# A two-layer Mish MLP on one core: x tiles 0 and 1 as two loads, w1's first eight f tiles as four loads by k, and k 0 by single x tiles

## The chip, the cores and the metric

The kernel runs on one core of a Trainium2 chip. Its engines are TensorE (PE, with PEld for its weight loads), VectorE (DVE), ScalarE (ACT), GpSimd (POOL) and SyncE (SP). SP and ACT each issue DMAs on a ring of their own; the transfers of both run on the same 16 DMA engines. The metric is the time of one execution in device microseconds (us), lower is better.

## The reference

All inputs are bf16: x is [1, 2048, 512], w1 [512, 1792], b1 [1792], w2 [1792, 512].

```
h   = einsum("bsd,df->bsf", x, w1) + b1
sp  = log1p(exp(-abs(h))) + where(h > 0, h, 0)
act = h * tanh(sp)                       # Mish
out = einsum("bsf,fd->bsd", act, w2)
```

## The kernel before

The 512 of the first contraction are four **k tiles** of 128, the 1792 hidden columns fourteen **f tiles** of 128, and the 2048 rows of x sixteen **x tiles** of 128, taken in four blocks of four. For every block the kernel computes h transposed (f on the partitions), `mm1_step` multiplying w1's tile (k, f) with the transposed x; ScalarE applies Mish with the bias and writes `a_sb`; `mm2` multiplies `a_sb` with w2 over the fourteen f tiles, VectorE copies the result to `o_sb` and SP stores it. The last tile's 512 output columns are cut into 416 and 96, the 96 copied and stored by ScalarE.

x has to be transposed. For x tiles 2 to 15 transposing loads do that (`load_xT`). Tiles 0 and 1 come as they are into `x_nat`, and TensorE transposes them against an identity, eight pieces of 128 x 128 into PSUM, from where VectorE copies them to `xT` (`transpose_x`). One load brings both tiles, with two neighbouring rows of x on each partition, so 2 KB in one piece; the output rows of tiles 0 and 1 are taken in that interleaving (`x01`, `out01`).

The order on every engine is the order in which the program is written; `Stream.wait` puts a semaphore wait in front of the next instruction of an engine, and `Stream.mark` makes an instruction count up. SP issues the load of x, then w1's f tiles 0 to 3 and 4 to 7 (`GROUPS`), each as a load of k 0 and 1 and one of k 2 and 3, in pieces of 1 KB; the very first of those goes on ScalarE's ring instead, behind a wait for VectorE's memset of `b1_pad`. ScalarE then issues the load of b1. On SP follow xT for x tiles 2 and 3, w1's f tiles 8 to 13, w2, and xT of the other blocks. No load waits for anything.

TensorE begins with dummy matmuls on constants (`WARM`: five of 512 columns, five of 128) into PSUM bank 7. Then come the transposes (k 0, k 1, k 2 and 3, for both x tiles at once), then f tiles 0 to 3 and after them 4 to 7, k outermost in either group, each step with the 256 columns of x tiles 0 and 1; each f tile has a PSUM bank of its own number. Then the same eight f tiles with x tiles 2 and 3, f outermost, with Mish behind each; then f tiles 8 to 13 with 512 columns, `mm2` of block 0, and the other blocks.

Of the kernel before, what the change touches and what calls it, by code (L numbers as in the profile page):

```python
# [4 lines left out]

P = 128
WARM = (512,) * 5 + (128,) * 5
GROUPS = ((0, 4), (4, 8), (8, 14))
BLOCKS = (512, 512, 512, 512)
LAST = 96  # L10

# [22 lines left out]
def bass_standalone__dense_activation_mish__prompt_kernel(  # L34
# [10 lines left out]
    BF, F32 = dt.bfloat16, dt.float32  # L45
# [3 lines left out]
    KT, FT = D // P, F // P  # L49
    assert (S, D, F) == (2048, 512, 1792) and sum(BLOCKS) == S  # L50
    x2, out2 = x[0], out[0]
# [3 lines left out]
    F0 = 8  # L55

    with ExitStack() as es:
        def sb(name, shape, t):
            return es.enter_context(nc.sbuf_tensor(name, shape, t))

        x_nat = sb("x_nat", [P, 2, D], BF)
        xT = sb("xT", [P, KT, S], BF)
# [7 lines left out]
        ident = sb("ident", [P, P], BF)  # L70
        a_sb = sb("a_sb", [P, FT, S], BF)
        o_sb = sb("o_sb", [P, S // P, D], BF)
        ps = es.enter_context(nc.psum_tensor("ps", [P, 8, 512], F32))

        def sem(name):
            return es.enter_context(nc.semaphore(name))

        sp = Stream(nc.sync, None)
        pe = Stream(nc.tensor, sem("c_pe"))
        dve = Stream(nc.vector, sem("c_dve"))  # L80
        act = Stream(nc.scalar, sem("c_act"))
        pool = Stream(nc.gpsimd, sem("c_pool"))

        def load(q, dst, src, name, transpose=False):
            s = sem(name)
            (q.eng.dma_start_transpose if transpose else q.eng.dma_start)(dst, src).then_inc(s, 16)
            return (s, 16)

        t_w1, t_w2, t_xT = {}, {}, {}

        def load_w1(q, ks, a, b):
            t = load(q, w1_sb[:, ks, a * P:b * P], w1v[:, ks, a * P:b * P], "s_w1_%d_%d" % (ks.start, a))
            for f in range(a, b):
                for k in range(ks.start, ks.stop):
                    t_w1[k, f] = t

        def load_w2(a, b):
            t = load(sp, w2_sb[:, a:b, :], w2v[:, a:b, :], "s_w2_%d" % a)
            for f in range(a, b):
                t_w2[f] = t  # L100

        def load_xT(lo, hi):
            t = load(sp, xT[:, :, lo:hi], x2[lo:hi, :], "s_xT%d" % lo, True)
            for j in range(lo // P, hi // P):
                t_xT[j] = t

        t_bz = dve.mark(nc.vector.memset(b1_pad[:, :], 0.0))  # L107
        act.wait(t_bz)

        x01 = x2[0:2 * P, :].rearrange("(p j) d -> p j d", j=2)  # L110
        out01 = out2[0:2 * P, :].rearrange("(p j) d -> p j d", j=2)
        t_xn = load(sp, x_nat[:, :, :], x01, "s_xn")
        for a, b in GROUPS:
            if a == F0:
                load_xT(2 * P, 4 * P)
            for ks in (slice(0, 2), slice(2, KT)):
                load_w1(act if (a, ks.start) == (0, 0) else sp, ks, a, b)
        t_b1 = load(act, b1_nat[:, :], b1.rearrange("(j p) -> j p", p=P), "s_b1")
        load_w2(0, 5)
        load_w2(5, FT)  # L120
        for s in range(1, len(BLOCKS)):
# [4 lines left out]
        t_id = pool.mark(pool.eng.affine_select(ident[:, :], ones[:, :], pattern=[[1, P]], compare_op=ALU.is_equal,  # L126
                                                fill=0.0, base=0, channel_multiplier=-1))
# [5 lines left out]
        def dummy(n):  # L133
            nc.tensor.matmul(ps[:, 7, 0:n], c_w, c_m[:, 0:n], start=True, stop=True)  # L134

        free = [[] for _ in range(8)]
        t_cp = {}
        t_mish = {}


        def transpose_x(bank, ks):
            pe.wait(t_xn, t_id, *free[bank])
            psb = ps[:, bank, :].bitcast(BF)
            for i, k in enumerate(ks):
                for j in range(2):
                    mm = nc.tensor.transpose(psb[:, (2 * i + j) * P:(2 * i + j + 1) * P],  # L146
                                             x_nat[:, j, k * P:(k + 1) * P], ident[:, :])
            n = len(ks)
            dve.wait(pe.mark(mm))
            t = dve.mark(nc.vector.tensor_copy(xT[:, ks[0]:ks[0] + n, 0:2 * P],  # L150
                                               psb[:, 0:2 * n * P].rearrange("p (k t) -> p k t", k=n)))
            for k in ks:
                t_cp[k] = t
            free[bank] = [t]

        def mm1_step(s, f, k, bank, j0=0, j1=None):
            j1 = BLOCKS[s] // P if j1 is None else j1
            lo, hi = j0 * P, j1 * P
            first = k == 0 and j0 == 0
            if first:  # L160
                pe.wait(*free[bank])
            pe.wait(t_w1[k, f])
            for j in range(starts[s] // P + j0, starts[s] // P + j1):
                pe.wait(t_cp[k] if j < 2 else t_xT[j])
            return nc.tensor.matmul(ps[:, bank, lo:hi], w1_sb[:, k, f * P:(f + 1) * P],  # L165
                                    xT[:, k, starts[s] + lo:starts[s] + hi], start=first,
                                    stop=(k == KT - 1 and hi == BLOCKS[s]))
# [8 lines left out]
        s_out = sem("s_out")  # L176
        n_out = 0

        def put(i, lo, hi, bank, t_mm, q):
            nonlocal n_out  # L180
            if q is act:
                act.wait(t_mm)
                t = act.mark(act.eng.activation(o_sb[:, i, lo:hi], ps[:, bank, 0:hi - lo], ACT.Copy))  # L183
            else:
                dve.wait(t_mm)
                t = dve.mark(nc.vector.tensor_copy(o_sb[:, i, lo:hi], ps[:, bank, 0:hi - lo]))  # L186
            free[bank] = [t]
            q.wait(t)
            dst = out01[:, i, lo:hi] if i < 2 else out2[i * P:(i + 1) * P, lo:hi]
            q.eng.dma_start(dst, o_sb[:, i, lo:hi]).then_inc(s_out, 16)  # L190
            n_out += 1

        def mm2(i, lo, hi, bank, q=sp):
            s = max(b for b in range(len(BLOCKS)) if starts[b] <= i * P)
            pe.wait(*free[bank])
            for f in range(FT):
                pe.wait(t_w2[f], t_mish[s, f])
                mm = nc.tensor.matmul(ps[:, bank, 0:hi - lo], a_sb[:, f, i * P:(i + 1) * P], w2_sb[:, f, lo:hi],  # L198
                                      start=(f == 0), stop=(f == FT - 1))
            put(i, lo, hi, bank, pe.mark(mm), q)  # L200


        for n in WARM:
            dummy(n)
        transpose_x(6, (0,))
        transpose_x(5, (1,))
        transpose_x(4, (2, 3))
        dve.wait(t_b1, t_bz)
        t_b1p = dve.mark(nc.vector.tensor_copy(b1_pad[0:FT, :], b1_nat[:, :]))  # L209
        dve.wait(t_b1p)  # L210
# [1 line left out]
            t_b1t = dve.mark(nc.vector.transpose(b1_t[c * 32:(c + 1) * 32, :], b1_pad[:, c * 32:(c + 1) * 32]))  # L212
        dve.wait(t_b1t)
        t_b1c = dve.mark(nc.vector.tensor_copy(b1_sb[:, :], b1_t[:, 0:FT]))  # L214
        for a, b in GROUPS[:2]:
            for k in range(KT):
                for f in range(a, b):
                    mm1_step(0, f, k, f, 0, 2)
        for f in range(F0):
            for k in range(KT):  # L220
                mm = mm1_step(0, f, k, f, 2, 4)
            mish(0, f, f, pe.mark(mm))

        for s in range(len(BLOCKS)):
            for f in range(F0 if s == 0 else 0, FT):
                bank = f % 8 if s == 0 else 4 + f % 4
                for k in range(KT):
                    mm = mm1_step(s, f, k, bank)
                mish(s, f, bank, pe.mark(mm))
            for i in range(starts[s] // P, starts[s + 1] // P):  # L230
                if i < S // P - 1:
                    mm2(i, 0, D, i % 4)
                else:
                    mm2(i, 0, D - LAST, i % 4)
                    mm2(i, D - LAST, D, (i + 1) % 4, act)
# [29 lines left out]
```

## Time and profile before

| what | value |
|---|---|
| median of 3 runs | 105.43 us (105.28 to 105.50) |
| the profiled execution, own time | 105.59 us |
| its span, first to last instruction | 104.3 us |
| TensorE busy | 101.6 us, 97% of the span, 512 matmuls |
| ScalarE busy | 38.9 us (37%) |
| VectorE busy | 13.2 us (13%) |
| DMA | 7.94 MB in all |

The profiled execution's own time is 1.3 us longer than its span: that lies around the first and the last instruction. Busy times of TensorE include the time in which a matmul drains while the next one already runs, so a duration is more than the distance from one matmul to the next; the distance is read from counts in a stretch, or from how the duration grows with the columns. All times in rows are microseconds from the start of the span unless they are marked ns.

### The profile page before, as it was taken

The page shows a single profiled execution, that of the slowest core. Times are in us where ns is not written, and L with a number is a line of the kernel's source. Part 1 is how long each engine was busy: PE and PEld are TensorE (multiplying, and loading weights), DVE is VectorE, ACT ScalarE, POOL GpSimd, SP SyncE. Part 2 cuts the span into 40 slices and gives each one's busy share as a digit, 9 for nine tenths or more (in the row PEclk, how much of TensorE's full clock was granted, in tenths as well). Part 3 has the DMA queues.
Part 4 walks back from the last instruction along what each step waited for, and adds up shares of the span by engine and source line. Part 5 has one row for each costly group of instructions (what it writes and reads, how often), then busy time and mean ns, then how long its engine had stood idle before and what let it go on. Part 6 is the DMA issues. An engine that isn't in the chain of part 4 may idle for free.

```text
span 104.3 us, 1168 instructions
## 1 busy us (share of the span) xinstructions
PE 101.6 (97%) x512; PEld 50.0 (48%) x512; DVE 13.2 (13%) x26; ACT 38.9 (37%) x58; POOL 0.7 (1%) x6
## 2 busy tenths in 40 slices
PE   6999999999999999999999999999999999999992
PEld 2689744444444444444444444444444444444452
DVE  0340000022220000022220000022112000021222
ACT  1303998000027777200007777500005777700000
POOL 2000000000000000000000000000000000000000
PEclk9999999999999999999999999999999999999999
DMA  2999999981101000010111000001111000001111
GB/s 48 360 296 356 351 257 142 258 202 50 37 14 50 0 0 6 0 49 1 50 50 50 0 0 0 9 0 50 50 50 50 0 0 0 0 6 50 50 50 50
DMA packets 13377, 7.94 MB, mean 76 GB/s; under 512 B 7868, under 2 KB 13244, under 8 KB 13372
## 3 DMA queue, kind: packets, MB, share of 16 engines
q1 hardware_dynamic: 12928, 7.58, 27.6%
q10 hardware_dynamic: 444, 0.29, 0.9%
q8 instruction: 4, 0.07, 0.3%
q14 instruction: 1, 0.01, 0.0%
HBM read 3.94 MB, written 2.10 MB: 58 GB/s over the span
## 4 chain that ended last, share of the span: by engine, by line
PE 97%; ACT 0%; issue 0%
PE ps L165 47%; PE ps L198 46%; PE ps L134 3%; PE ps L146 1%; ACT o_sb L183 0%
## 5 line engine op out<-in xcount | busy, mean ns | idle before, releaser
L171 ACT ACTIVATE a_sb<-ps,b_sb 128x512 bf16<-128x512 f32 x56 | 37.4, 693 | 50.1 <-PE ps L165 50.1
L165 PE MATMUL ps<-xT,w_sb 128*128 128x512 bf16 (+1 forms) x256 | 50.0, 357 | 0.0
L198 PE MATMUL ps<-w_sb,a_sb 128*128 128x512 bf16 (+2 forms) x238 | 49.0, 366 | 0.0
L165 PEld LDWEIGHTS ps<-xT,w_sb 128*128 128x128 bf16 x256 | 25.4, 100 | 23.6
L198 PEld LDWEIGHTS ps<-w_sb,a_sb 128*128 128x128 bf16 x238 | 22.6, 98 | 26.1
L186 DVE CAST o_sb<-ps 128x512 bf16<-128x512 f32 (+1 forms) x16 | 11.0, 685 | 84.8 <-PE ps L198 84.8
L183 ACT ACTIVATE o_sb<-ps 128x96 bf16<-128x96 f32 x1 | 0.3, 251 | 11.4 <-PE ps L198 11.4
L134 PE MATMUL ps<-const-bfloat16-1.0 128*128 128x512 bf16 (+1 forms) x10 | 2.8, 469 | 0.8 <-PEq L250 0.8
L134 PEld LDWEIGHTS ps<-const-bfloat16-1.0 128*128 128x128 bf16 x10 | 1.2, 142 | 2.2 <-issue 2.2
L128 ACT ACT_TABLE_LOAD x1 | 1.3, 1283 | 2.2 <-issue 2.2
L150 DVE COPY xT<-ps 128x256 bf16<-128x256 bf16 (+1 forms) x3 | 0.9, 336 | 3.2 <-PE ps L146 3.1
L146 PE MATMUL ps<-ident,x_nat 128*128 128x128 bf16 x8 | 1.0, 311 | 0.0
L146 PEld LDWEIGHTS ps<-ident,x_nat 128*128 128x128 bf16 x8 | 0.8, 142 | 0.3 <-DMA x_nat<-in_x_dram 0.3
L212 DVE STREAM_TRANSPOSE b_t<-b_pad 32x32 bf16<-32x32 bf16 x4 | 0.8, 202 | 0.1
L126 POOL TENSOR_SCALAR_AFFINE_SELECT ident<-ones 128x128 bf16<-128x128 bf16 x1 | 0.3, 294 | 0.1
L107 DVE MEMSET b_pad<- 32x64 uint32 x1 | 0.1, 112 | 0.9 <-PEq L250 0.9
L124 POOL MEMSET ones<- 128x128 bf16 x1 | 0.2, 205 | 0.3 <-POOLq L250 0.3
L209 DVE COPY b_pad<-b_nat 14x128 bf16<-14x128 bf16 x1 | 0.2, 182 | 0.2 <-DMA b_nat<-in_b_dram 0.2
L214 DVE CAST b_sb<-b_t 128x14 f32<-128x14 bf16 x1 | 0.2, 175 | 0.0
L250 POOL MEMSET const-bfloat16-1.0<- 128x1 bf16 x1 | 0.1, 102 | 0.0
L250 POOL MEMSET const-uint8-127<- 128x1 uint8 x1 | 0.1, 102 | 0.0
L250 POOL MEMSET const-float32-0.0<- 128x1 f32 x1 | 0.1, 99 | 0.3 <-issue 0.3
(1 smaller groups left out, 0.1 us busy)
## 6 DMA issues: line engine op xcount, KB each, us to landing
out_dram<-o_sb SPq DMA_DIRECT2D x15, 128.0 KB, 1.7
w_sb<-in_w_dram SPq DMA_DIRECT2D x1, 1152.0 KB, 10.1
w_sb<-in_w_dram SPq DMA_DIRECT2D x3, 256.0 KB, 4.2
w_sb<-in_w_dram SPq DMA_DIRECT2D x2, 384.0 KB, 5.4
w_sb<-in_w_dram SPq DMA_DIRECT2D x1, 640.0 KB, 7.2
x_nat<-in_x_dram SPq DMA_DIRECT2D x1, 256.0 KB, 2.8
w_sb<-in_w_dram ACTq DMA_DIRECT2D x1, 256.0 KB, 3.4
out_dram<-o_sb SPq DMA_DIRECT2D x1, 104.0 KB, 1.7
```

The lines of the kernel that those rows point to most:

```text
L126: t_id = pool.mark(pool.eng.affine_select(ident[:, :], ones[:, :], pattern=[[1, P]], compare_op=ALU.is_equal, fill=0.0, base=0, channel_mu ...
L128: act.eng.preload_act_table(ACT.Mish)
L134: nc.tensor.matmul(ps[:, 7, 0:n], c_w, c_m[:, 0:n], start=True, stop=True)
L146: mm = nc.tensor.transpose(psb[:, (2 * i + j) * P:(2 * i + j + 1) * P], x_nat[:, j, k * P:(k + 1) * P], ident[:, :])
L150: t = dve.mark(nc.vector.tensor_copy(xT[:, ks[0]:ks[0] + n, 0:2 * P], psb[:, 0:2 * n * P].rearrange("p (k t) -> p k t", k=n)))
L165: return nc.tensor.matmul(ps[:, bank, lo:hi], w1_sb[:, k, f * P:(f + 1) * P], xT[:, k, starts[s] + lo:starts[s] + hi], start=first, stop=( ...
L171: t = act.mark(act.eng.activation(a_sb[:, f, starts[s]:starts[s + 1]], ps[:, bank, 0:BLOCKS[s]], ACT.Mish, bias=b1_sb[:, f:f + 1]))
L183: t = act.mark(act.eng.activation(o_sb[:, i, lo:hi], ps[:, bank, 0:hi - lo], ACT.Copy))
L186: t = dve.mark(nc.vector.tensor_copy(o_sb[:, i, lo:hi], ps[:, bank, 0:hi - lo]))
L198: mm = nc.tensor.matmul(ps[:, bank, 0:hi - lo], a_sb[:, f, i * P:(i + 1) * P], w2_sb[:, f, lo:hi], start=(f == 0), stop=(f == FT - 1))
L212: t_b1t = dve.mark(nc.vector.transpose(b1_t[c * 32:(c + 1) * 32, :], b1_pad[:, c * 32:(c + 1) * 32]))
L250: nc = _bacc.Bacc("TRN2", target_bir_lowering=False, num_devices=1)
```

## The change

x tiles 0 and 1 come as two loads on SP's ring, tile by tile, each with one row of x (1 KB) on a partition; the output rows of tiles 0 and 1 are then plain rows as those of the others. w1's f tiles 0 to 7 come as four loads, one for each k, in pieces of 2 KB: k 0 on ScalarE's ring, k 1 to 3 on SP's. `GROUPS` goes. `transpose_x` takes one x tile at a time and copies in four parts instead of three: x0's k 0, x0's k 1 to 3, x1's k 0, x1's k 1 to 3, in banks 4 to 7. Of the five dummies of 128 columns one is left (`GAP`), between the transposes of x0 and of x1. The steps on x tiles 0 and 1 run k outermost over all eight f tiles; k 0 runs over the eight f tiles with x0 alone (128 columns) and then with x1 alone, k 1 to 3 with both (256 columns).

```diff
-WARM = (512,) * 5 + (128,) * 5
-GROUPS = ((0, 4), (4, 8), (8, 14))
+WARM = (512,) * 5
+GAP = (128,)
...
-        x01 = x2[0:2 * P, :].rearrange("(p j) d -> p j d", j=2)
-        out01 = out2[0:2 * P, :].rearrange("(p j) d -> p j d", j=2)
-        t_xn = load(sp, x_nat[:, :, :], x01, "s_xn")
-        for a, b in GROUPS:
-            if a == F0:
-                load_xT(2 * P, 4 * P)
-            for ks in (slice(0, 2), slice(2, KT)):
-                load_w1(act if (a, ks.start) == (0, 0) else sp, ks, a, b)
+        def load_x(j):
+            t_xn[j] = load(sp, x_nat[:, j, :], x2[j * P:(j + 1) * P, :], "s_xn%d" % j)
+
+        load_x(0)
+        load_x(1)
+        for k in range(KT):
+            load_w1(sp if k else act, slice(k, k + 1), 0, F0)
         t_b1 = load(act, b1_nat[:, :], b1.rearrange("(j p) -> j p", p=P), "s_b1")
+        load_xT(2 * P, 4 * P)
+        for ks in (slice(0, 2), slice(2, KT)):
+            load_w1(sp, ks, F0, FT)
...
-        def transpose_x(bank, ks):
-            pe.wait(t_xn, t_id, *free[bank])
-            psb = ps[:, bank, :].bitcast(BF)
+        def transpose_x(j, bank, ks):
+            pe.wait(t_xn[j], t_id, *free[bank])
+            psb = ps[:, bank, 0:2 * P].bitcast(BF)
             for i, k in enumerate(ks):
-                for j in range(2):
-                    mm = nc.tensor.transpose(psb[:, (2 * i + j) * P:(2 * i + j + 1) * P],
-                                             x_nat[:, j, k * P:(k + 1) * P], ident[:, :])
+                mm = nc.tensor.transpose(psb[:, i * P:(i + 1) * P], x_nat[:, j, k * P:(k + 1) * P], ident[:, :])
...
-        transpose_x(6, (0,))
-        transpose_x(5, (1,))
-        transpose_x(4, (2, 3))
+        transpose_x(0, 4, (0,))
+        transpose_x(0, 5, (1, 2, 3))
+        for n in GAP:
+            dummy(n)
+        transpose_x(1, 6, (0,))
+        transpose_x(1, 7, (1, 2, 3))
...
-        for a, b in GROUPS[:2]:
-            for k in range(KT):
-                for f in range(a, b):
-                    mm1_step(0, f, k, f, 0, 2)
+        for j in range(2):
+            for f in range(F0):
+                mm1_step(0, f, 0, f, j, j + 1)
+        for k in range(1, KT):
+            for f in range(F0):
+                mm1_step(0, f, k, f, 0, 2)
```

TensorE's first rows, from the start of the program to the second block's first product; a minus is the kernel before, a plus the changed one (L134 and L135 are the dummies, L146 the transposes, L165 and L164 the steps on w1):

```order
-L134 MATMUL ps<-const-bfloat16-1.0 128x512 x5
-L134 MATMUL ps<-const-bfloat16-1.0 128x128 x5
-L146 MATMUL ps<-ident,x_nat 128x128 x8
-L165 MATMUL ps<-xT,w_sb 128x256 x64
...
+L135 MATMUL ps<-const-bfloat16-1.0 128x512 x5
+L146 MATMUL ps<-ident,x_nat 128x128 x4
+L135 MATMUL ps<-const-bfloat16-1.0 128x128
+L146 MATMUL ps<-ident,x_nat 128x128 x4
+L164 MATMUL ps<-xT,w_sb 128x128 x16
+L164 MATMUL ps<-xT,w_sb 128x256 x56
```

The transposes are in two parts with a dummy between them, and eight steps of 256 columns have become sixteen of 128.

What TensorE waits for there in the changed kernel (s_xn0 and s_xn1 are the loads of x0 and x1, s_w1_0_0 to s_w1_3_0 those of w1's k 0 to 3, c_dve the copies of VectorE):

```order
2 L146 MATMUL ps<-ident,x_nat 128x128 [waits c_pool,s_xn0]
3 L146 MATMUL ps<-ident,x_nat 128x128 x3
4 L135 MATMUL ps<-const-bfloat16-1.0 128x128
5 L146 MATMUL ps<-ident,x_nat 128x128 [waits s_xn1]
6 L146 MATMUL ps<-ident,x_nat 128x128 x3
7 L164 MATMUL ps<-xT,w_sb 128x128 [waits c_dve,s_w1_0_0]
8 L164 MATMUL ps<-xT,w_sb 128x128 x4
9 L164 MATMUL ps<-xT,w_sb 128x128 [waits c_dve] x3
10 L164 MATMUL ps<-xT,w_sb 128x128 x8
```

The wait for x1 stands ahead of every step on w1.

SP's first rows, the loads in the order of issue, before and after:

```order
-L86 DMA x_nat<-in_x_dram 128x1024
-L86 DMA w_sb<-in_w_dram 128x2x512 x3
+L86 DMA x_nat<-in_x_dram 128x512 x2
+L86 DMA w_sb<-in_w_dram 128x1024 x3
 L86 DMA_TRANSPOSE xT<-in_x_dram 128x4x256
 L86 DMA w_sb<-in_w_dram 128x2x768 x2
```

One load more stands ahead of xT's first, and the second place on the ring is x1's.

## Rows read from the trace of the kernel before

**Rows 1.** The page's busy times, us (share of the span) xinstructions.
```profile
PE 101.6 (97%) x512; PEld 50.0 (48%) x512; DVE 13.2 (13%) x26; ACT 38.9 (37%) x58; POOL 0.7 (1%) x6
```
**Rows 2.** The chain that ended last, pieces in order: start, length, what.
```profile
0.84 2.83 PE ps L134 x10
...
4.70 13.06 PE ps L165 x88
17.75 12.09 PE ps L198 x56
...
90.28 12.14 PE ps L198 x70
```
**Rows 3.** Who waited for whom: the one wait of TensorE for data.
```profile
PEld ps L146 <- DMA x_nat<-in_x_dram: 0.3, 1, 0.3
```
**Rows 4.** Timeline of the DMA issues on SP and ACT: start, length, line, operation.
```profile
0.81 0.39 SPq L86 DMA_DIRECT2D x_nat<-in_x_dram  x1
1.02 0.43 ACTq L86 DMA_DIRECT2D w_sb<-in_w_dram  x1
1.26 0.41 SPq L86 DMA_DIRECT2D w_sb<-in_w_dram  x1
1.72 0.46 SPq L86 DMA_DIRECT2D w_sb<-in_w_dram  x1
...
2.74 1.30 SPq L86 DMA_TRANSPOSE xT<-in_x_dram  x1
```
**Rows 5.** DMA issues, same order, and two stores: KB, us from issue to landing.
```profile
x_nat<-in_x_dram SPq DMA_DIRECT2D x1, 256.0 KB, 2.8
w_sb<-in_w_dram ACTq DMA_DIRECT2D x1, 256.0 KB, 3.4
w_sb<-in_w_dram SPq DMA_DIRECT2D x1, 256.0 KB, 3.9
w_sb<-in_w_dram SPq DMA_DIRECT2D x1, 256.0 KB, 4.2
...
xT<-in_x_dram SPq DMA_TRANSPOSE x1, 5.0
...
out_dram<-o_sb SPq DMA_DIRECT2D x15, 128.0 KB, 1.7
out_dram<-o_sb ACTq DMA_DIRECT2D x1, 24.0 KB, 1.6
```
**Rows 6.** TensorE's timeline around the transposes: the last dummy, transposes, first steps.
```profile
3.35 0.31 PE L134 MATMUL ps<-const-bfloat16-1.0 128*128 128x128 bf16 x1
3.66 1.03 PE L146 MATMUL ps<-ident,x_nat 128*128 128x128 bf16 x8
...
4.53 2.04 PE L165 MATMUL ps<-xT,w_sb 128*128 128x256 bf16 x9
```
**Rows 7.** By line and form, PE to 6.39, DVE to 7: busy us, mean ns.
```profile
L134 PE MATMUL ps<-const-bfloat16-1.0 128*128 128x512 bf16 x5 | 2.3, 624 | 0.8 <-PEq L250 0.8
L165 PE MATMUL ps<-xT,w_sb 128*128 128x256 bf16 x9 | 2.0, 411 | 0.0
...
L150 DVE COPY xT<-ps 128x256 bf16<-128x256 bf16 x2 | 0.5, 292 | 3.1 <-PE ps L146 3.1
L150 DVE COPY xT<-ps 128x512 bf16<-128x512 bf16 x1 | 0.4, 423 | 0.1
```
**Rows 8.** Stretches, L165 alone: length, PE busy (count), PEld, granted clock, DMA share, GB/s.
```profile
4.53:6.40 1.87, 1.87 (x9) 1.33 (x10) 1.00 1.15 337
6.40:8.02 1.62, 1.62 (x17) 1.46 (x15) 1.00 1.14 291
```
**Rows 9.** A stretch, PE: length, busy (count), granted clock, DMA share, GB/s.
```profile
1.75:2.50 0.75, 0.75 (x4) 1.00 0.90 134
```
**Rows 10.** Timeline: the last step on b1, and the first Mish.
```profile
6.48 0.17 DVE L214 CAST b_sb<-b_t 128x14 f32<-128x14 bf16 x1
...
9.62 0.69 ACT L171 ACTIVATE a_sb<-ps,b_sb 128x512 bf16<-128x512 f32 x1 [6.12 <-PE ps L165]
```

More of the change, by code (lines that the diff above doesn't have):

```diff
@@ L87, in load @@
             return (s, 16)
-        t_w1, t_w2, t_xT = {}, {}, {}
+        t_xn, t_w1, t_w2, t_xT = [None] * 2, {}, {}, {}
         def load_w1(q, ks, a, b):
@@ L138, in bass_standalone__dense_activation_mish__prompt_kernel @@
         t_mish = {}
-        def transpose_x(bank, ks):
-            pe.wait(t_xn, t_id, *free[bank])
-            psb = ps[:, bank, :].bitcast(BF)
+        def transpose_x(j, bank, ks):
+            pe.wait(t_xn[j], t_id, *free[bank])
+            psb = ps[:, bank, 0:2 * P].bitcast(BF)
             for i, k in enumerate(ks):
-                for j in range(2):
-                    mm = nc.tensor.transpose(psb[:, (2 * i + j) * P:(2 * i + j + 1) * P],
-                                             x_nat[:, j, k * P:(k + 1) * P], ident[:, :])
+                mm = nc.tensor.transpose(psb[:, i * P:(i + 1) * P], x_nat[:, j, k * P:(k + 1) * P], ident[:, :])
             n = len(ks)
             dve.wait(pe.mark(mm))
-            t = dve.mark(nc.vector.tensor_copy(xT[:, ks[0]:ks[0] + n, 0:2 * P],
-                                               psb[:, 0:2 * n * P].rearrange("p (k t) -> p k t", k=n)))
+            t = dve.mark(nc.vector.tensor_copy(xT[:, ks[0]:ks[0] + n, j * P:(j + 1) * P],
+                                               psb[:, 0:n * P].rearrange("p (k t) -> p k t", k=n)))
             for k in ks:
-                t_cp[k] = t
+                t_cp[j, k] = t
             free[bank] = [t]
@@ L163, in mm1_step @@
             for j in range(starts[s] // P + j0, starts[s] // P + j1):
-                pe.wait(t_cp[k] if j < 2 else t_xT[j])
+                pe.wait(t_cp[j, k] if j < 2 else t_xT[j])
             return nc.tensor.matmul(ps[:, bank, lo:hi], w1_sb[:, k, f * P:(f + 1) * P],
@@ L188, in put @@
             q.wait(t)
-            dst = out01[:, i, lo:hi] if i < 2 else out2[i * P:(i + 1) * P, lo:hi]
-            q.eng.dma_start(dst, o_sb[:, i, lo:hi]).then_inc(s_out, 16)
+            q.eng.dma_start(out2[i * P:(i + 1) * P, lo:hi], o_sb[:, i, lo:hi]).then_inc(s_out, 16)
             n_out += 1
```

## The prediction

> **What bounds the kernel now.** Read the head of the page first: TensorE is busy 101.6 us, 97% of the span of 104.3 [rows 1]. Then the chain that ended last: from the first warm-up matmul at 0.84 us to 102.4 us it is TensorE, piece upon piece, with no other engine in between until the last copy [rows 2]. Such a chain says that only three things can move the end: TensorE's work itself, the level of its clock, and the holes in it. So the third view is the table of waits, and in it TensorE waits once on data: 0.3 us for x, ahead of the transposes [rows 3]. Everything that the change touches lies ahead of 9 us; the 90 us behind it are the same instructions in the same order, fed by loads that this chain does not wait for.
>
> The clock needs care, since the granted clock reads 1.00 in every stretch [rows 8], and yet there are two levels. A matmul's duration grows from 411 to 624 ns between 256 and 512 columns before 6.4 us (213 ns for 256 columns: 1.2 GHz) [rows 7]; later 56 matmuls of 512 columns follow each other in 12.09 us, 108 ns for 256 columns (2.4 GHz) [rows 2]. Counts agree: 9 matmuls of 256 columns touch the 1.87 us before 6.40, 17 touch the next 1.62 us [rows 8]. So TensorE runs at the lower level from 0.84 to about 6.40 us, and all that time it stood still only from the end of the last dummy's columns (3.35 + 0.11 = 3.46) to the first transpose at 3.66 [rows 6]. It follows that **a microsecond lost before 6.40 costs half a microsecond at the end**, provided the clock rises at the same moment: the columns not done by then are done later in 108 instead of 213 ns per 256.
>
> What the first matmul on w1 (4.53) waits for: x lands at 0.81 + 2.8 = 3.61, eight transposes fill 3.66 to 4.53 (0.87), and w1's first 256 KB from ScalarE's ring land at 1.02 + 3.4 = 4.42 [rows 4 to 6]. The two are nearly tied. From there the loads are ahead: w1's next parts land at 5.16 and 5.92, xT's at 7.74 [rows 4, 5].
>
> **The change, part by part.** *Dummies.* Five dummies of 128 columns go from ahead of x (5 x 107 = 0.53 us at the lower level), one stays between the transposes. They stood in front of the wait for x, so they buy nothing by themselves; without them TensorE is free from about 0.84 + 5 x 0.426 = 2.97 on.
>
> *x in two loads.* x0 is 128 KB and first in line. Loads that queue behind each other land 0.74 to 0.76 us apart per 256 KB (4.42, 5.16, 5.92), so 128 KB less is 0.37 us earlier at the full rate; the first stretch, 1.75 to 2.50, moved only 134 GB/s against 337 later [rows 8, 9], and that start is not halved by halving the load. I bound x0's landing between 3.61 - 0.37 = 3.24 and 3.61 and take 3.37. Four transposes run 3.42 to 3.85, the dummy to 3.96. Before, nothing of this was done by then but what began at 3.66.
>
> *x1.* This is the term that decides. It is SP's second load, issued at about 1.25, where the second SP load stood before; ScalarE's load is issued at 1.02, ahead of it. In the trace the landings go by the order of issue across both rings: x (issued 0.81), ScalarE's w1 (1.02), SP's w1 (1.26), SP's w1 (1.72) [rows 4, 5]. So I expect x0, k 0, x1: 128 + 256 + 128 KB ahead of and with x1, which is just what had moved when ScalarE's w1 landed at 4.42. x1 lands at 4.42 less what 2 KB rows give (k 0 and k 1 to 3 have 128 pieces of 2 KB for 256 of 1 KB; no row prices them alone, x itself had such rows; I take 0 to 0.1 us, 0.05). But the transposes of x1 stand in TensorE's order ahead of *every* matmul on w1, also of those on x0. TensorE therefore waits from 3.96 to about 4.42 (0.46 us), then 0.05 from landing to start (3.61 to 3.66) and 4 transposes, 0.43: the first matmul on w1 at 4.85 to 4.90, against 4.53. **That is 0.34 us later, at the lower level, so 0.17 us at the end.** What is late next is nothing: k 1 to 3 land at about 5.1, 5.9 and 6.6 while k 0 alone keeps TensorE 16 x 107 = 1.71 us, to 6.6.
>
> *Sixteen matmuls of 128 for eight of 256 columns.* Same columns, eight more instructions and weight loads. At the lower level the transposes show 128 columns with a weight load of their own each in (0.87 / 8) 109 ns, half of 213, so nothing. At the higher level the last block tells it: 14 pairs of 416 + 96 columns made a piece of the chain 12.14 us long where whole ones take 12.09 [rows 2], 4 ns a pair, so 8 x 4 = 0.03 us at most. Since most of k 0 runs before 6.40, I take 0; range 0 to 0.03. The Trainium skill (TensorE: Matmul & The Clock Gate, section Back-to-back issue gap) speaks against such a split: it gives about 81 ns for each pair of weight load and matmul at 128 columns. By that 16 of them would be an estimated 1.30 us instead of 0.87 at the higher level and the sum 0.4 us worse, were the stage run there; the row with the 96-column pairs shows no such floor, so the measurement decides.
>
> *Four copies out of PSUM for three.* Copies of 256 columns take 292 ns, of 512, 423 [rows 7], so 128 columns about 0.23 and 384 about 0.36. The last (x1, k 1 to 3) starts when the last transpose has ended, 0.31 us after its start, and is done about 0.6 us after the first matmul. It frees bank 7, which the eighth matmul needs 7 x 107 = 0.75 us in: covered by 0.15 us. If TensorE ran at the higher level there the cover would be gone and 0.2 us waited. The b1 steps on VectorE follow later by about 0.3 us and end near 6.9 instead of 6.65; the first Mish starts at 9.62 [rows 10], so nothing.
>
> *Queues.* SP has six loads instead of five ahead of xT's transposing load, about 0.45 us more issue: it is issued at 3.2 instead of 2.74. Its bytes wait behind the same 1.25 MB anyway, and it lands at 7.74 to 8.2; its first reader comes after all steps on tiles 0 and 1, near 8.9 (6.40 + 23 x 0.108). Nothing, with 0.7 us of cover. Outputs of tiles 0 and 1 go to whole rows; their issue is far off the chain. Nothing.
>
> **The sum.** 0.17 (0.12 to 0.20) + 0 to 0.03: on the profiled execution 105.59 + 0.17 = 105.76. The median of the runs is 105.43, 0.16 below it, so 105.60.
>
> **The rivals.** *A. The clock rises later (slower).* Before, TensorE stood still 0.2 us between its start and the rise at 6.40. Now it stands still from 2.97 to 3.42 and from 3.96 to 4.47, nearly 1.0 us. Nothing in this trace says how much stillness the rise bears. Each microsecond of delay costs 0.5 us. The bounds: none, or the account starts anew at 4.47 and takes the 5.56 us that lay between 0.84 and 6.40, so that the rise comes at 10.0, 3.6 us later: 1.8 us, 107.4. For it: both holes stand in the stretch right before the rise. Against it: neither hole is longer than 0.5 us, and the old kernel had one too. It decides from the point where the rise moves by 0.1 us (with the 0.17 us above it passes 0.2%).
>
> *B. x1 lands before k 0.* If SP's two loads are served first, x1 lands near 3.37 + 0.37 = 3.75 and its transposes end at 4.4; k 0 lands at 4.37 and the first matmul is at 4.43: 0.10 us earlier, 0.05 at the end, 105.4. For it: nothing shows when ScalarE's request is ready, only that it was served second. Against it: that order itself.
>
> *C. Loads come faster.* If the slow start is one of bytes and not of time, x0, k 0 and x1 all land up to 0.4 us earlier; the first matmul is at 4.45 to 4.5, level with before, 105.4, or with B at 4.0, 105.15. The 2 KB rows of x, the slow stretch's own, speak against it.
>
> *D. Each load pays its own start.* A store of 24 KB took 1.6 us and one of 128 KB 1.7 [rows 5]: nearly all start. Were x1's start not hidden behind k 0, x1 would land up to 1.5 us later, the first matmul come at 6.4, and 0.93 us be lost: 106.4. Landings 0.74 us apart say that starts hide. The Trainium skill (DMA: Bandwidth & Descriptors, section Bandwidth) has the rule behind this rival, to batch loads toward 1 MiB; the spacing of the landings does not bear it out here.
>
> **How the numbers follow.** Forecast 0.41, its own range 105.4 to 105.8; A 0.33; B 0.16; C 0.06; D 0.04. A measurement tells about 0.2% (0.21 us) from no change. The forecast's 0.17 us lies close to that: 0.27 of its 0.41 within, 0.14 slower. B gives 0.13 within and 0.03 faster, C 0.02 and 0.04, A and D slower. Sum: faster 0.07, same 0.42, slower 0.51. The likeliest single case is the forecast, 105.60. The range must take in A and B: 105.2 to 107.4.
>
> **What would show it.** In the trace after: x0's landing 3.3 to 3.4; TensorE's two waits for x, the second of 0.4 to 0.5 us; ScalarE's k 0 landing before x1; first matmul on w1 at 4.8 to 4.9; the change from 213 to 108 ns per 256 columns at 6.4 (forecast) or later (A); the chain all TensorE from there. A first matmul before 4.6 makes the forecast wrong by B or C; a rise past 6.6 by A; a wait of TensorE for k 1 to 3 or xT by something that I have not priced.

## The result, and the profile after

The changed kernel takes 105.51 us (median of 19 runs, 105.11 to 105.81), the kernel before 104.93 beside it (19 runs, 104.56 to 105.63): a ratio of 1.0038, interval 1.0019 to 1.0056, so 0.40 us slower (0.20 to 0.59); the two medians lie 0.58 us apart. The forecast of 105.60 was near the time and had the sign; it had 0.17 us of the loss, and not for the reason that the trace shows.

The runs themselves say something that the medians hide. The slowest are nearly alike, the quickest are missing:

```
                    lowest  median  highest   runs under 105.0
before (19 runs)    104.56  104.93  105.63    11
changed (19 runs)   105.11  105.51  105.81     0
```

The chain that ended last, of the kernel after (start, length, what), answers to [rows 2]:

```profile
1.72 0.42 SPq L86
2.15 0.04 issue
2.19 4.88 DMA w_sb<-in_w_dram
7.07 0.05 issue
7.12 10.59 PE ps L164 x72
17.71 12.09 PE ps L196 x56
...
90.23 12.14 PE ps L196 x70
```

Before, this chain was TensorE from 0.84 us on. Now it begins as a load: SP's fourth load, k 2, issued at 2.19 and landed at 7.07. TensorE is the chain only from there. TensorE's timeline (start, length, line, form, and the idle time ahead with what ended it) shows two holes, and answers to [rows 6]:

```profile
2.98 0.61 PE L146 MATMUL ps<-ident,x_nat 128*128 128x128 bf16 x4
3.38 0.31 PE L135 MATMUL ps<-const-bfloat16-1.0 128*128 128x128 bf16 x1
4.16 0.61 PE L146 MATMUL ps<-ident,x_nat 128*128 128x128 bf16 x4 [0.46 <-DMA x_nat<-in_x_dram]
4.56 2.38 PE L164 MATMUL ps<-xT,w_sb 128*128 128x128 bf16 x24
7.12 1.05 PE L164 MATMUL ps<-xT,w_sb 128*128 128x256 bf16 x8 [0.17 <-DMA w_sb<-in_w_dram]
```

The bracket counts from the modelled end of a draining matmul; counted from the end of the last matmul's columns ("by the columns" from here on) the first hole is 0.67 us (3.49 to 4.16) and the second 0.34 (6.78 to 7.12). The first was forecast, for x1. The second is new: 24 steps, all of k 0 and k 1, run without a break, and then k 2 is not there.

The DMA issues (KB, us to landing), in the order of issue at 0.81, 1.02, 1.26, 1.72, 2.19 and 2.66, answer to [rows 5]:

```profile
x_nat<-in_x_dram SPq DMA_DIRECT2D x1, 128.0 KB, 2.1
w_sb<-in_w_dram ACTq DMA_DIRECT2D x1, 256.0 KB, 2.7
x_nat<-in_x_dram SPq DMA_DIRECT2D x1, 128.0 KB, 2.9
w_sb<-in_w_dram SPq DMA_DIRECT2D x1, 256.0 KB, 3.5
w_sb<-in_w_dram SPq DMA_DIRECT2D x1, 256.0 KB, 4.9
w_sb<-in_w_dram SPq DMA_DIRECT2D x1, 256.0 KB, 5.1
```

x0 lands at 2.91, k 0 at 3.72, x1 at about 4.11, just ahead of its transposes (the order forecast, earlier than forecast), then k 1 at 5.22, k 2 at 7.07, k 3 at 7.76. In the kernel before, the third and fourth of w1's loads had landed at 5.92 [rows 4, 5] and 6.73. What happened in between is one row of the table of stretches (length, PE busy and count, granted clock, DMA share, GB/s). The kernel after:

```profile
3.60:4.20 0.60, 0.14 (x2) 1.00 1.04 371
4.20:5.00 0.80, 0.80 (x9) 1.00 0.78 120
5.00:6.00 1.00, 1.00 (x15) 1.00 0.87 312
```

The kernel before, same stretch:

```profile
4.20:5.00 0.80, 0.80 (x8) 1.00 1.07 369
```

For 0.8 us the loads move 120 GB/s where they moved 369. I call this the dip, and the late landing of k 2 and k 3 the lag; the experiments show that the two do not always come together.

The clock rose at another time in this trace. Steps alone (L164; length, PE busy and count, PEld, granted clock, DMA share, GB/s):

```profile
4.60:5.40 0.80, 0.80 (x8) 0.80 (x9) 1.00 0.72 197
5.55:5.91 0.36, 0.36 (x9) 0.36 (x8) 1.00 0.81 313
```

Eight steps of 128 columns touch 0.80 us, then nine touch 0.36: the rise lies near 5.5, not at 6.40. That is worth 0.45 us by the half-price rule of the prediction, the hole at k 2 costs 0.34 of it again, and so the two traced spans are equal, 104.3, by accident.

### The profile page after: what moved, and what is told of

It is laid out like the page before. It is cut to its first block, busy times and chain, and to the rows that moved or that the text cites. A ratio compares the mean times of both kernels' runs of the same rounds, so it can differ in the third digit from the quotient of the medians.

```text
span 104.3 us, 1177 instructions
## 1 busy us (share of the span) xinstructions
PE 100.9 (97%) x516; PEld 49.4 (47%) x516; DVE 13.3 (13%) x27; ACT 38.9 (37%) x58; POOL 0.7 (1%) x6
## 4 chain that ended last, share of the span: by engine, by line
PE 91%; DMA 5%; SPq 1%; issue 0%; ACT 0%
PE ps L196 46%; PE ps L164 45%; DMA w_sb<-in_w_dram 5%; SPq L86 1%; ACT o_sb L182 0%
## 5 line engine op out<-in xcount | busy, mean ns | idle before, releaser
L164 PE MATMUL ps<-xT,w_sb 128*128 128x512 bf16 (+2 forms) x264 | 49.7, 350 | 0.2 <-DMA w_sb<-in_w_dram 0.2
L164 PEld LDWEIGHTS ps<-xT,w_sb 128*128 128x128 bf16 x264 | 25.5, 100 | 23.6 <-DMA w_sb<-in_w_dram 0.5
L135 PE MATMUL ps<-const-bfloat16-1.0 128*128 128x512 bf16 (+1 forms) x6 | 2.6, 571 | 0.8 <-PEq L253 0.8
L146 PE MATMUL ps<-ident,x_nat 128*128 128x128 bf16 x8 | 1.2, 308 | 0.5 <-DMA x_nat<-in_x_dram 0.5
L149 DVE COPY xT<-ps 128x128 bf16<-128x128 bf16 (+1 forms) x4 | 1.2, 290 | 3.0 <-PE ps L146 2.8
L135 PEld LDWEIGHTS ps<-const-bfloat16-1.0 128*128 128x128 bf16 x6 | 0.7, 133 | 1.6 <-issue 1.6
L146 PEld LDWEIGHTS ps<-ident,x_nat 128*128 128x128 bf16 x8 | 0.7, 131 | 1.5 <-DMA x_nat<-in_x_dram 1.5
## 6 DMA issues: line engine op xcount, KB each, us to landing
out_dram<-o_sb SPq DMA_DIRECT2D x1, 104.0 KB, 1.7
```

Of the source, the lines that this page charges most:

```text
L146: mm = nc.tensor.transpose(psb[:, i * P:(i + 1) * P], x_nat[:, j, k * P:(k + 1) * P], ident[:, :])
L149: t = dve.mark(nc.vector.tensor_copy(xT[:, ks[0]:ks[0] + n, j * P:(j + 1) * P], psb[:, 0:n * P].rearrange("p (k t) -> p k t", k=n)))
```

## The experiments

Every ratio is against the kernel before, run beside the kernel in question; its median there lay between 104.93 and 105.20, so ratios compare better than times do. Two theories stood at first. **L**: the loads lag and TensorE waits for k 2; in its first form, because of w1's 2 KB pieces. **C**: the landing of 7.07 belongs to one execution, and the hole between the transposes moves the rise of the clock.

**The changed kernel again.** No edit.

> The changed kernel once more, for a second trace. In its first trace TensorE stood still twice: 0.67 us between the transposes of x0 and x1, and 0.34 us before the first step of k 2, whose load landed at 7.07 (the same 256 KB lay at 5.91 to 6.73 in the kernel before). Theory L (the loads): w1 by k in 2 KB pieces comes in late whatever the run; k 2 lands at 6.5 or later again, TensorE waits for it 0.2 us or more if its clock has risen by 5.6, and the time is near 105.5 against 104.9 before. Theory C (the clock): the landing of 7.07 belongs to that one execution, k 2 lands near 6.0 here, and the time is still 105.3 to 105.6, because the hole between the transposes moves the rise of the clock.

105.52 (12 runs, 104.77 to 105.83), ratio 1.0032 (1.0002 to 1.0062). k 2 landed at 2.19 + 4.5 = 6.69, k 3 at 7.36; 205 GB/s from 4.20 to 5.00. The clock rose near 4.8, and TensorE lost 0.16 us ahead of the eighth step and 0.08 on k 2. The first of these waits is not for a load (engine, line, what it waited for: us in all, times, longest):

```profile
PEld ps L164 <- DVE xT L149: 0.2, 1, 0.2
```

The eighth step writes bank 7, which the last copy of x1 frees; at the higher level the prediction had priced this wait at 0.2 us. The dip is no matter of one execution, though its size varies. C's first half falls. One of these twelve runs, 104.77, is as quick as the quick ones of the kernel before: 1 of 31 with the first nineteen.

**Only x changed.** Against the changed kernel, w1's loads and steps go back to those of before:

```diff
-        for k in range(KT):
-            load_w1(sp if k else act, slice(k, k + 1), 0, F0)
+        for a, b in GROUPS:
...
+            for ks in (slice(0, 2), slice(2, KT)):
+                load_w1(act if (a, ks.start) == (0, 0) else sp, ks, a, b)
...
-        for j in range(2):
-            for f in range(F0):
-                mm1_step(0, f, 0, f, j, j + 1)
+        for a, b in GROUPS[:2]:
+            for k in range(KT):
+                for f in range(a, b):
+                    mm1_step(0, f, k, f, 0, 2)
```

> Only x is changed: two loads, transposes tile by tile with the one dummy between them; w1's loads and steps as before (1 KB pieces, two groups of four f tiles, 256 columns). The hole between the transposes stays, the 2 KB pieces of w1 go. Theory L: no wait of TensorE for w1, 104.8 to 105.0, as the kernel before. Theory C: 105.3 to 105.6, as the changed one.

107.59 (6 runs, 106.80 to 107.88), ratio 1.0217 (1.0178 to 1.0256): outside both. TensorE's timeline of this kernel:

```profile
3.35 0.31 PE L136 MATMUL ps<-const-bfloat16-1.0 128*128 128x128 bf16 x1
4.57 0.61 PE L147 MATMUL ps<-ident,x_nat 128*128 128x128 bf16 x4 [0.90 <-DMA x_nat<-in_x_dram]
5.26 3.93 PE L165 MATMUL ps<-xT,w_sb 128*128 128x256 bf16 x18
```

and its steps in two stretches (columns as above):

```profile
5.20:8.95 3.75, 3.69 (x18) 2.60 (x19) 1.00 1.13 275
9.02:11.00 1.98, 1.98 (x21) 1.77 (x19) 1.00 1.08 366
```

18 steps of 256 columns in 3.75 us, then 21 in 1.98: the clock rises only at 9.0. Ahead of that TensorE had stood still 1.10 us for x1 (which lands at 4.52 here) and 0.30 for the copies of x1, since a step of 256 columns needs both tiles. The first step is 0.73 us late and the rise 2.6: half of 3.3 is 1.65, and its span of 106.0 is 1.7 us longer than before. This is rival A of the prediction, in a kernel where the holes are larger. In the changed kernel the rise is not that late, in either trace.

The stretch in which the changed kernel has its dip:

```profile
4.20:5.00 0.80, 0.43 (x4) 1.00 1.05 365
```

There is no dip in it; this trace has an earlier one, 115 GB/s from 2.50 to 3.00, where the kernel before moved 311. And the third and fourth of w1's loads land at 2.19 + 4.3 = 6.49 and 2.70 + 4.5 = 7.20, 0.57 and 0.47 us later than in the kernel before: the lag is there with the loads of w1 as they were. TensorE, still at the lower level, does not wait for them.

**Only w1 changed.** Against the kernel before, whose x, transposes and dummies stay:

```diff
-        for a, b in GROUPS:
...
-            for ks in (slice(0, 2), slice(2, KT)):
-                load_w1(act if (a, ks.start) == (0, 0) else sp, ks, a, b)
+        for k in range(KT):
+            load_w1(sp if k else act, slice(k, k + 1), 0, F0)
...
-        for a, b in GROUPS[:2]:
-            for k in range(KT):
-                for f in range(a, b):
-                    mm1_step(0, f, k, f, 0, 2)
+        for k in range(KT):
+            for f in range(F0):
+                mm1_step(0, f, k, f, 0, 2)
```

> Only w1 is changed: four loads by k in 2 KB pieces, k 0 on ScalarE's ring, steps k outermost over eight f tiles with 256 columns; x as before in one load, all ten dummies. No hole between the transposes. Theory L: k 2 lands at 6.4 or later and TensorE waits for it, 105.3 to 105.6. Theory C: no hole, so 104.8 to 105.0.

104.94 (12 runs, 104.55 to 105.79, seven under 105.0), ratio 0.9995 (0.9965 to 1.0024). Its stretch (columns as above):

```profile
4.20:5.00 0.80, 0.45 (x5) 1.00 1.04 354
```

and its steps in the timeline:

```profile
4.58 3.67 PE L164 MATMUL ps<-xT,w_sb 128*128 128x256 bf16 x32 [0.35 <-DMA w_sb<-in_w_dram]
```

No dip, and once k 0 has landed 32 steps in one piece, though the clock had risen already near 3.7 and the steps ran at 109 ns each: the loads keep up with the higher level. w1 by k in 2 KB pieces, k outermost, costs nothing and gives nothing. L in its first form falls: the lag comes with the change of x, which by itself also had it. The dip from 4.20 to 5.00 shows in neither of the two kernels with only one half of the change.

**w1 by k in 1 KB pieces.**

```diff
+        w1_h = sb("w1_h", [P, KT, 2, 544], BF)
...
+                t = load(q, w1_h[:, k, :, 0:512], w1[k * P:(k + 1) * P, 0:F0 * P].rearrange("p (h c) -> p h c", h=2), ...)
```

> The changed kernel with each of the four loads of w1 in 1 KB pieces (the two halves of a k's 1024 columns lie 64 bytes apart on chip), everything else the same: same bytes, order, loads and steps. Theory L with the size of the pieces as its cause: k 1 to 3 land near 5.0, 5.8 and 6.5, no wait for k 2, 104.9 to 105.1. Theory L with another cause (the order of the loads): k 2 late as in the changed kernel, 105.5. Theory C: 105.3 to 105.6, whatever the landings.

105.54 (12 runs, 105.08 to 106.82), ratio 1.0031 (1.0010 to 1.0052). The dip stays (206 GB/s), k 2 lands at 2.19 + 4.8 = 6.99 and TensorE, at the higher level since about 4.3, loses 0.22 us ahead of the eighth step, for the copy of x1, and 0.60 on k 2. The size of w1's pieces is not the cause.

So the second round set C against **D**: the dip, with its own cause to be found.

**The hole filled.**

```diff
-GAP = (128,)
+GAP = (128,) * 6
```

> The changed kernel with six dummies of 128 columns in place of one between the transposes of x0 and x1, so that TensorE works from 2.9 to about 4.1 and the hole of 0.67 us shrinks to 0.1; loads, order and steps untouched. Theory C (the hole moves the rise of the clock): the time falls to 104.9 to 105.1. Theory D (a dip in the loads: in three traces of the changed kernel and its 1 KB form they moved 70 to 240 GB/s from 4.2 to 5.0, where the kernel before moved 370, and k 2 landed at 6.7 to 7.07): the hole is not what costs, k 2 lands at 6.6 or later as ever and the time stays at 105.4 to 105.6.

105.53 (12 runs, 105.25 to 105.90), ratio 1.0052 (1.0030 to 1.0074). The timeline shows the hole gone, its place taken by dummies:

```profile
3.18 0.61 PE L146 MATMUL ps<-ident,x_nat 128*128 128x128 bf16 x4
3.58 0.84 PE L135 MATMUL ps<-const-bfloat16-1.0 128*128 128x128 bf16 x6
4.22 0.63 PE L146 MATMUL ps<-ident,x_nat 128*128 128x128 bf16 x4
```

k 2 lands at 6.69 and the stretch moves 238 GB/s. The time does not change: the hole of 0.67 us is not what the changed kernel pays for. C falls for this kernel.

**x1 ahead of k 0.**

```diff
...
-        load_x(0)
-        load_x(1)
-        for k in range(KT):
-            load_w1(sp if k else act, slice(k, k + 1), 0, F0)
+        load_x(0, sp)
+        load_x(1, act)
+        for k in range(KT):
+            load_w1(sp, slice(k, k + 1), 0, F0)
```

> The changed kernel with x1 on ScalarE's ring and k 0 as SP's second load, so that x0, x1, k 0 is the order of issue. x1 should land near 3.3, its transposes follow x0's without a hole, k 0 lands near 4.15 and the first step on w1 starts at 4.2 instead of 4.56. Theory C: 104.7 to 104.9 (no hole, and 0.36 us less at the lower level). Theory D: TensorE comes to k 1 and k 2 sooner and waits there for longer; if the dip stays, 105.3 to 105.5; if the dip belongs to the order of the loads, 104.7.

105.58 (12 runs, 104.76 to 105.96), ratio 1.0050 (1.0027 to 1.0073). The first step on w1 comes at 4.26, 0.3 us earlier than in the changed kernel, and the median does not move. The trace is of the quickest run, 104.76: the clock rose near 4.8, k 2 landed at 2.19 + 4.0 = 6.19, and TensorE lost no more than 0.06 us on k 1 to 3. The dip has moved: 228 GB/s from 3.60 to 4.20, 333 after it.

> e5_order (x0, x1, k 0 in the order of issue) once more. Its median was 105.58 and its one trace of an execution of 104.76, with k 2 at 6.20 and no wait of TensorE for k 1 to 3. If a lag of the loads is what the median shows, a trace of an execution near the median has k 1 at 5.4 or later and k 2 at 6.4 or later with waits of TensorE for them of 0.5 us in all or more. If it is the clock, such a trace has no such waits and the rise of the clock at 6 or later.

The same kernel again: 105.55 (12 runs, 104.79 to 106.00), ratio 1.0040 (1.0012 to 1.0068). The traced execution is one of 105.40. Its stretch:

```profile
3.60:4.20 0.60, 0.60 (x7) 1.00 0.73 183
```

and its steps in the timeline:

```profile
4.05 1.76 PE L164 MATMUL ps<-xT,w_sb 128*128 128x128 bf16 x16
6.05 2.14 PE L164 MATMUL ps<-xT,w_sb 128*128 128x256 bf16 x18 [0.25 <-DMA w_sb<-in_w_dram]
```

The first step starts 0.48 us earlier than in the kernel before; then TensorE stands 0.41 us (by the columns) until k 1 lands at 1.72 + 4.3 = 6.02. The clock rose near 5.5. That is less waiting than the expectation named for the lag and an earlier rise than it named for the clock. It speaks for the lag without settling its whole size.

**SP held before the transposing load.**

```diff
+        sp.wait(t_w1[1, 0])
         load_xT(2 * P, 4 * P)
```

> The changed kernel, with SP held before the transposing load of x tiles 2 and 3 until w1's k 1 has landed (near 5.2), so that this load and all behind it are issued after 5.2 instead of from 3.14 on. Where the dip comes from SP's issue of the transposing load (3.14 to 4.45, just ahead of the dip), k 2 and k 3 land at 5.9 and 6.7 and TensorE doesn't wait for k 2; xT then lands at 9.5 or later and TensorE waits for it, so the time is no better, 105.5 to 106.5. Where the dip has another cause, k 2 lands at 6.6 or later all the same.

105.63 (10 runs, 105.41 to 105.93), ratio 1.0066 (1.0043 to 1.0090). 256 GB/s in the stretch, with no transposing load issued before 5.85, and k 2 at 2.18 + 4.3 = 6.48. The dip is shallower and it stays: SP's issue of the transposing load is not its cause, or not alone. TensorE waits 0.45 us for xT instead.

**k 0 in steps of 256 columns.**

```diff
-        for j in range(2):
-            for f in range(F0):
-                mm1_step(0, f, 0, f, j, j + 1)
-        for k in range(1, KT):
+        for k in range(KT):
```

> The changed kernel with k 0 in eight steps of 256 columns over both x tiles instead of sixteen of 128; loads and transposes as changed. The first step then waits for the copy of x1's k 0, to about 4.75. Where the dip comes from TensorE's narrow steps (a weight load every 107 ns from 4.56 on), k 2 lands near 6.0 and the time is 104.9 to 105.2. Otherwise k 2 lands at 6.6 or later and the time is 105.4 to 105.7.

106.83 (6 runs: 105.45, 105.51, 106.78, 106.88, 106.89, 107.64), ratio 1.0124 (1.0068 to 1.0180). The dip stays (164 GB/s; k 2 at 2.18 + 4.9 = 7.08), so narrow steps don't make the dip. The runs fall in two groups, and the trace, of 106.89, is of the upper one. Its timeline:

```profile
4.09 0.61 PE L146 MATMUL ps<-ident,x_nat 128*128 128x128 bf16 x4 [0.42 <-DMA x_nat<-in_x_dram]
4.79 4.47 PE L164 MATMUL ps<-xT,w_sb 128*128 128x256 bf16 x22
```

and its steps in two stretches:

```profile
5.20:8.60 3.40, 3.40 (x18) 2.42 (x17) 1.00 1.14 228
8.77:11.00 2.23, 2.23 (x23) 2.01 (x21) 1.00 1.07 367
```

TensorE stood still 0.63 us for x1 and 0.29 for its copies, and the clock rose at 8.7. The narrow steps of the changed kernel start on x0 while x1 is copied, 0.29 us of stillness less, and none of its 31 runs is above 105.83. So the sixteen narrow steps look worth having, once x1 comes late; that it is the stillness that moves the rise rests on two traces.

**What of x's loads.** The last three start from the kernel with only w1 changed (104.94, ratio 0.9995), in which TensorE transposes both tiles as before, and change x's loads alone.

One load, but in 1 KB pieces:

```diff
-        x01 = x2[0:2 * P, :].rearrange("(p j) d -> p j d", j=2)
+        x01 = x2[0:2 * P, :].rearrange("(j p) d -> p j d", p=P)
```

> The kernel with only w1 changed (e2_w1_by_k, 104.94) but x, still in one load, in 1 KB pieces, one row of either tile on a partition, as the changed kernel has its rows. Theory R (the 1 KB rows of x make the loads behind it lag): k 2 lands at 6.5 or later, time 105.4 to 105.6. Theory N (that x comes as two loads does it): no lag, k 2 near 5.8, time 104.8 to 105.1.

105.43 (12 runs, 104.64 to 105.92), ratio 1.0021 (0.9993 to 1.0049): undecided by the time. In its trace, at the higher level from about 4.0, k 2 lands at 1.81 + 4.8 = 6.61 and TensorE stands 0.21 us for it: the lag that theory R expected and N did not. From 4.20 to 5.00 it moves 320 GB/s, so this is a lag without a dip as well.

Two loads, 2 KB pieces, one on either ring, k 0 behind them on SP's:

```diff
-        t_xn = load(sp, x_nat[:, :, :], x01, "s_xn")
+        t_xn = load(sp, x_nat[0:64, :, :], x01[0:64, :, :], "s_xn")
+        t_xm = load(act, x_nat[64:P, :, :], x01[64:P, :, :], "s_xm")
```

> The kernel with only w1 changed (e2_w1_by_k, 104.94) but x as two loads of 64 partitions each, in the old 2 KB pieces, one on SP's ring and one on ScalarE's, k 0 second on SP's, so that the order of issue is x, x, k 0, k 1, as in e5_order; TensorE still waits for both and does the same. Theory N: the loads behind lag, k 2 at 6.2 or later, 105.3 to 105.6. Theory R: no lag, k 2 near 5.8, 104.8 to 105.1.

105.73 (12 runs, 105.54 to 106.19), ratio 1.0060 (1.0033 to 1.0087).

Two loads, tile by tile in 1 KB pieces:

```diff
+        t_xn = load(sp, x_nat[:, 0, :], x01[:, 0, :], "s_xn")
+        t_xm = load(act, x_nat[:, 1, :], x01[:, 1, :], "s_xm")
```

> As e9_two_2kb, but the two loads are x tile 0 and x tile 1 in 1 KB pieces, as in e5_order; transposes and steps are those of e2_w1_by_k. Theories N and R both expect the lag here: k 2 at 6.2 or later, 105.3 to 105.6. If the time is 104.8 to 105.1 both fall, and the lag comes from what TensorE does tile by tile and not from x's loads.

105.42 (12 runs, 105.20 to 105.99), ratio 1.0035 (1.0010 to 1.0060). The steps in the timeline of the kernel with 2 KB pieces:

```profile
4.76 1.30 PE L165 MATMUL ps<-xT,w_sb 128*128 128x256 bf16 x8
6.50 1.70 PE L165 MATMUL ps<-xT,w_sb 128*128 128x256 bf16 x14 [0.44 <-DMA w_sb<-in_w_dram]
```

and of the one with 1 KB pieces, tile by tile:

```profile
4.36 1.29 PE L165 MATMUL ps<-xT,w_sb 128*128 128x256 bf16 x8
6.27 1.92 PE L165 MATMUL ps<-xT,w_sb 128*128 128x256 bf16 x16 [0.62 <-DMA w_sb<-in_w_dram]
```

Both run the eight steps of k 0 and then stand, 0.60 and 0.78 us by the columns, until k 1 has landed at 6.45 and 6.22, where the kernel they start from had it at 5.2. With TensorE's work untouched, x in two loads brings the lag back, in pieces of either size; from 4.20 to 5.00 both move 312 GB/s, against the dip's 120 to 256. The lag doesn't need that dip. So R falls as the only cause, by the two loads in 2 KB pieces, and so does N, by the one load in 1 KB pieces: x in the old form, one load in 2 KB pieces, is the only one here without the lag.

## Why the prediction was right, and where it was not

*The time and the sign* were right: 105.51 for 105.60, slower. That the time came so near is luck. The forecast stands on a median of 105.43 from three runs; nineteen gave 104.93, 0.50 us less, and the loss forecast, 0.17 us, is under half of 0.40. The two errors cancel: from 104.93 the same sum gives 105.10, below the stated range.

*x0, x1 and the first step.* The order x0, k 0, x1 held in every trace of the changed kernel. The landings were taken too late: x0 at 2.91 (2.80 in the second trace) for 3.37, x1 at about 4.11 (4.17) for 4.37. I had taken the slow start as one of time; half the load landed 0.70 us sooner than the whole one had, as rival C allowed. So the first step on w1 came at 4.56 (4.62) and not at 4.85: the term of 0.34 us measured 0.03 to 0.09, the 0.17 us at the end 0.02 to 0.05. By the prediction's own sign, a first matmul before 4.6, the first trace makes it wrong by B or C, and as k 0 landed ahead of x1 it is C, which had a chance of 0.06 and would have left the time level. The loss has another source.

*"What is late next is nothing"* is the step that failed. It carried the spacing of [rows 5], 0.74 us per 256 KB, over to loads behind a different start. k 1 was to land at 5.1, k 2 at 5.9, k 3 at 6.6; they landed at 5.22, 7.07 and 7.76, and at 6.69 and 7.36 for k 2 and k 3 in the second trace. None of the four rivals has late loads of w1; the closing list named a wait for k 1 to 3 as what had not been priced, and that is what came.

*A clock that rises at 6.40* was the second fault, and it hid the first. In twelve of the fourteen traces it rises between 3.7 and 6.4 us, and at different times in two executions of one kernel (5.5 and 4.8 in the changed one). With a late rise TensorE needs k 2 no sooner than it comes: the hole-filled kernel, risen near 5.8, did not wait for it at 6.69. With an early one the kernel before would gain half a microsecond per microsecond, down to its 104.56, and the changed kernel reaches the landing of k 2 and stands. That would be the table of runs at the top: nearly equal at the slow end, hardly a quick end. It also fits that the changed kernel, its 1 KB form, the filled hole and x1 ahead of k 0 all have medians of 105.5 to 105.6, though their first steps lie between 4.05 and 4.65. That an early rise is what the quick runs of the kernel before have in common is an inference: its one trace has a late rise and a time of 105.59.

Three terms bear it out in all fourteen traces: the start of the first step on w1, half of the time from there to the rise, and what TensorE stands still after that first step. The kernel before has 4.53 + 0.94 + 0 = 5.47, the changed one 4.56 + 0.47 + 0.34 = 5.37, its second trace 4.62 + 0.09 + 0.24 = 4.95, the kernel with only w1 changed 4.58, x1 ahead of k 0 in its quick trace 4.26 + 0.25 + 0.06 = 4.57, and w1 in 1 KB pieces 4.47 + 0 + 0.82 = 5.29. The spans, 104.3, 104.3, 104.0, 103.5, 103.5 and 104.3, are longer than these sums by 98.8 to 99.1 us, as are the other eight. So the quick traces have an early rise and hardly a wait, and the 1 KB form, which rises early as well, loses it all to waits. An estimate from these rows: k 0 and k 1 take 1.7 us at the higher level, so with k 2 there at 6.69 to 7.07 the changed kernel's sum cannot fall much below 5.0 to 5.4, where 4.53 is open to the kernel before. That is a floor higher by 0.5 to 0.9 us; the lowest runs of the nineteen differ by 0.55.

*The narrow steps* at no cost: right, and better than that, as the kernel with 256 columns showed. *The four copies*: as priced. In the first trace, still at the lower level there, no stop at the eighth step; where the clock had risen by then, the 0.2 us forecast for that case came, 0.16 us in the second trace and 0.22 with w1 in 1 KB pieces. *The queues*: xT landed at 3.14 + 5.7 = 8.8, past the 8.2 allowed, and nothing waited for it. SP has five loads ahead of it where four were, not six and five, and from a first step at 4.87 some 25 steps would be left at 6.40 and not 23; neither count changes the sum.

*Rival A* was real in other kernels than the changed one: with 0.92 and 1.40 us of stillness ahead of it the rise came at 8.7 and 9.0 (the kernels with 256 columns and with only x changed), and their medians lie 1.3 and 2.1 us above the changed kernel's. After the 0.67 and 0.76 us of the changed kernel's two traces it did not come late, and none of its 31 runs is as slow.

**What stays open.** Which property of x's load sets the loads behind it back. Shown: not w1's piece size, not the order of w1's loads, not TensorE's steps, not the hole, not SP's transposing load alone; two loads for one bring the lag, in either piece size, with both on SP's ring or one on either, and in one trace one load in 1 KB pieces brings it too. One thing that the kernels with two loads share was not varied by itself: SP issues k 2 later, at 2.18 to 2.50, where the third of w1's loads had gone out at 1.72. It cannot be the whole cause, as the one load in 1 KB pieces had k 2 out at 1.81 and landed at 6.61. Why the dip comes where it does is open as well. Summed over the stretches, 138 thousand bytes had moved when it began with x alone changed (2.4 us), 535 and 552 with x1 ahead of k 0 (3.6), 794 in the changed kernel (4.4): close to one, three and four whole loads (131, 524 and 786 thousand bytes), as if the next one were not ready; no run tests that. Nothing here beat the kernel before; the one with only w1 changed ties with it.

## What to carry to other kernels

When a change touches the first loads, price the landing of every load behind them against the earliest moment at which the engine could ask for it, not against the moment in the one trace at hand: a clock that rises earlier asks earlier. Where a difference of medians puzzles, lay the sorted runs side by side: a missing quick end can be a floor, here a wait for a late load. And if a tile must arrive late, try narrower steps on the tile that is there: with 0.29 us filled by them none of 31 runs was in the slow group, without them four of six, 1.3 us at the median.

## What the runs showed of the hardware

With one load of 256 KB in 2 KB pieces at the head of the queue (the kernel before, and the one with only w1 changed) the last of w1's first four loads landed at 6.73 and 6.48; with two loads of 128 KB, or one in 1 KB pieces, it landed between 6.86 and 7.78, in twelve traces. In the changed kernel and its variants the rate also fell from some 370 GB/s to between 120 and 256 for 0.6 to 0.8 us; with only x changed the fall came earlier (115 GB/s from 2.50 to 3.00) and shorter, and the lag came all the same.

At the higher level a transpose of 128 columns with its own weight load takes 57 ns: in the kernel with only w1 changed eight of them start and drain in 0.62 us, one alone in 0.22, where at the lower level the changed kernel's four take 0.61, one alone 0.31, 100 ns apart. The roughly 81 ns for each pair of weight load and matmul at 128 columns that the Trainium skill states (TensorE: Matmul & The Clock Gate, section Back-to-back issue gap) does not show here. The transposes of the kernel with only w1 changed, in its timeline:

```profile
3.61 0.62 PE L145 MATMUL ps<-ident,x_nat 128*128 128x128 bf16 x8
```

and by line and form (busy us, mean ns of one):

```profile
L145 PE MATMUL ps<-ident,x_nat 128*128 128x128 bf16 x8 | 0.6, 220 | 0.0
```
